# The last 2,176 bytes a row of a weight load in loads of 126, 2, 124 and 4 rows, so that the sixteen DMA engines get unequal shares

## Chip, cores, metric

One core of a Trainium2 chip; nothing else of the program runs on the others. The metric is the device time of one execution in microseconds (us), slowest core; lower is better. Engines: PE is TensorE's matmul side, DVE is VectorE, ACT is ScalarE, SP is the sync engine that issues nearly all loads. "Engine 5" means DMA engine 5 of the core's sixteen. A straggler is an engine that finishes its share of the loads clearly later than most; the "body" are the engines that are none.

## The reference

A decoding step for 8 sequences: a modulation (six vectors of 1,024 from `silu(c) @ w_mod`), attention of 32 query heads over a cache of 8,192 keys in 4 groups, and a gated MLP. Cut to what matters here:

```python
mod = (silu(c) @ w_mod).reshape(8, 6, 1, -1)            # w_mod: 1024 x 6144 bf16, 12.6 MB
h = layernorm(x) * (1 + ca) + sa
x = x + ga * attention(h, k_cache, v_cache, wq, wo)     # caches: 2 x 67 MB, wq and wo: 8.4 MB each
h = layernorm(x) * (1 + cb) + sb
x = x + gb * ((relu(h @ W_gate) * (h @ W_up)) @ W_down) # 3 x 7.3 MB
```

There are 186 MB to read for very little arithmetic.

## The kernel before

All big inputs go through one ring in on-chip memory, `arena`, with 128 rows of 128 KB. A list of loads is made up front; each is issued from SP as soon as the program has read what stood in its place.

```python
def load(key, src, n, lo):
    place[key] = lo
    stream.append((key, src, n, lo))

def pump():
    while stream:
        key, src, n, lo = stream[0]
        if P.unread("arena", lo, lo + n):
            return
        stream.pop(0)
        dst = arena[:, lo:lo + n]
        P.op("sp", lambda e, dst=dst, src=src: e.dma_start(dst, src), writes=[slot_r(lo, lo + n)], dma=True, ...)
...
load(("wm", 0), wm_src[:, 0:D], D, 0)                     # D = 1024 columns of 2 bytes
load(("wm0", 0), wm_src[:, D:24 * D], 23 * D, D)
load(("wm", 1), wm_src[:, 24 * D:48 * D], 24 * D, 24 * D) # the load that is changed
... # wq in two loads; for each of 8 sequences K in two loads and V in one; wo, W_gate, W_up
wd_parts = [(0, 14), (14, 21), (21, 25), (25, 27), (27, 28)]
for i, (r0, r1) in enumerate(wd_parts):                   # W_down, in ever smaller loads
    load(("wd", i), d_src[:, r0 * D:r1 * D], (r1 - r0) * D, VPART + r0 * D)
```

Every load has 128 rows. The matmuls of the modulation read the ring in two halves; the second half waits for `("wm", 1)`. At the end each piece of W_down has its own matmuls, then two VectorE operations and the store follow.

## Time and profile before

| | before |
|---|---|
| three timed runs | 436.43, 436.43, 436.64 us |
| profiled run, its span | 444.49, 443.1 us (state: slow) |
| DMA engines' busy share of the span in the queue of the loads | 98.9% |
| busiest compute engines | PE 59%, DVE 56% |
| bytes read | 185.63 MB |

The profile of before fell in a slow execution, 8 us longer than the timed ones. The lines that carry the argument are in the prediction. Beside the page, I read the trace's records of single DMA packets (start, duration, bytes; no engine number) and of the sixteen steps by which a load's semaphore rises, one for each engine that has finished its share.

### The profile page before, as it was taken

The numbers are of one execution on the slowest core, as the hardware profiler recorded it, in microseconds if no ns is written. First come the engines' busy times: TensorE is split into PE (matmuls) and PEld (weight loads), VectorE is DVE, ScalarE is ACT, GpSimd is POOL, SyncE is SP. The second block draws the span as 40 slices with busy tenths as digits, with TensorE's granted clock in tenths as the row PEclk, the third lists the DMA queues.
The fourth block names the chain that finished last, engine by engine and source line by source line (L and its number), as shares of the span: only waits on it lengthen the run. The fifth ranks groups of instructions, "written<-read, shape, count | busy, mean of one in ns | idle before, by whom it ended". The sixth has DMA issues, their size and how long they took to land. (4 is left out here: it accounts for less than half of the span.)

```text
span 443.1 us, 4774 instructions
## 1 busy us (share of the span) xinstructions
PE 263.3 (59%) x2139; PEld 138.0 (31%) x1979; DVE 249.0 (56%) x342; ACT 29.5 (7%) x54; POOL 8.7 (2%) x22
## 2 busy tenths in 40 slices
PE   0324336728865783886578388658838865365157
PEld 0100002218225421822542172154217215241015
DVE  0603028872985697298569729756972975421020
ACT  1100010020001002000100200010020010100000
POOL 3000000000000000000000000000000000000000
PEclk9976657978996997799599889959968996865668
DMA  9999999999999999999999999999999999999995
GB/s 367 417 355 390 404 385 426 379 417 430 467 396 420 456 444 420 429 470 390 435 476 408 423 429 467 420 423 473 399 420 426 467 455 402 452 416 419 439 414 239
DMA packets 5494, 185.74 MB, mean 419 GB/s; under 512 B 656, under 2 KB 752, under 8 KB 1136
## 3 DMA queue, kind: packets, MB, share of 16 engines
q1 hardware_dynamic: 5360, 185.61, 98.9%
q8 instruction: 5, 0.08, 0.1%
q10 hardware_dynamic: 128, 0.04, 0.0%
q14 instruction: 1, 0.01, 0.0%
HBM read 185.63 MB, written 0.02 MB: 419 GB/s over the span
## 5 line engine op out<-in xcount | busy, mean ns | idle before, releaser
L576 DVE STREAM_TRANSPOSE kt<-arena 128x1024 uint32<-128x1024 uint32 x128 | 148.2, 1211 | 64.4 <-DVEq L181 47.3
L586 PE MATMUL ps<-kt,qpad 128*128 128x512 bf16 x512 | 133.9, 384 | 44.1 <-DVE kt L576 38.1
L626 PE MATMUL ps<-arena,pT 128*64 128x256 bf16 x1024 | 74.5, 320 | 51.8 <-PEq L181 51.8
L626 PEld LDWEIGHTS ps<-arena,pT 128*64 128x64 bf16 x1024 | 72.0, 132 | 53.7 <-issue 53.1
L586 PEld LDWEIGHTS ps<-kt,qpad 128*128 128x128 bf16 x512 | 40.5, 98 | 133.7 <-DVE kt L576 101.0
L616 DVE TENSOR_SCALAR pT<-pd,mqf 128x1024 bf16<-128x1024 bf16 x64 | 28.2, 503 | 0.6
L608 ACT ACTIVATE prb<-ps,bias 128x1024 bf16<-128x1024 f32 x16 | 17.7, 1109 | 139.8 <-DVE mjt L603 139.8
L614 DVE STREAM_TRANSPOSE pd<-prb 128x1024 bf16<-128x1024 bf16 x16 | 19.8, 1239 | 10.9 <-ACT prb L608 10.9
L592 DVE TENSOR_REDUCE negm<-ps 128x1 f32<-128x512 f32 x32 | 21.2, 661 | 4.5 <-PE ps L586 4.5
L744 PE MATMUL ps<-arena,hT 128*32 128x448 bf16 x128 | 11.1, 535 | 16.8 <-DMA arena<-in_B_W_up_dram 11.4
L751 DVE TENSOR_TENSOR kt<-ps,kt 128x448 bf16<-128x448 f32 x2 | 1.2, 618 | 27.6 <-PE ps L744 27.6
L514 PE MATMUL ps<-arena,hT 128*32 128x512 bf16 x96 | 10.3, 615 | 9.7 <-DMA arena<-in_w_mod_dram 9.7
L538 PE MATMUL ps<-arena,hT 128*32 128x512 bf16 x64 | 7.2, 631 | 14.6 <-DMA arena<-in_A_wq_dram 14.6
L645 ACT ACTIVATE oacc<-ps 128x32 f32 (+1 forms) x9 | 1.8, 197 | 159.4 <-PE ps L640 159.4
L521 DVE COPY mod<-ps 128x512 f32<-128x512 f32 x2 | 1.3, 670 | 19.3 <-PE ps L514 19.3
L567 POOL TENSOR_TENSOR qpad<-qR,mq 128x128 bf16<-128x128 bf16 x8 | 4.9, 608 | 319.2 <-DVE pT L616 260.8
L549 DVE CAST kt<-ps 128x512 bf16<-128x512 f32 x1 | 0.7, 691 | 18.2 <-PE ps L538 18.2
L744 PEld LDWEIGHTS ps<-arena,hT 128*32 128x32 bf16 x64 | 2.4, 140 | 25.7 <-DMA arena<-in_B_W_up_dram 12.0
L763 PE MATMUL ps<-arena,hmT 128*32 128x256 bf16 x112 | 8.3, 309 | 3.5 <-DVE hmT L754 3.1
L714 PE MATMUL ps<-arena,kt 128*32 128x256 bf16 x128 | 5.9, 373 | 5.1 <-DMA arena<-in_A_wo_dram 5.1
L598 PE MATMUL ps<-identf,negm 128*128 128x128 f32 x16 | 3.9, 326 | 7.8 <-DVE negm L596 7.8
L763 PEld LDWEIGHTS ps<-arena,hmT 128*32 128x32 bf16 x112 | 6.5, 109 | 5.6 <-DMA arena<-in_B_W_down_dram 4.9
(87 smaller groups left out, 80.9 us busy)
## 6 DMA issues: line engine op xcount, KB each, us to landing
arena<-in_A_k_cache_dram SPq DMA_DIRECT2D x16, 4096.0 KB, 27.5
arena<-in_A_wq_dram SPq DMA_DIRECT2D x2, 4096.0 KB, 38.3
arena<-in_B_W_gate_dram SPq DMA_DIRECT2D x1, 7168.0 KB, 24.7
arena<-in_B_W_up_dram SPq DMA_DIRECT2D x1, 7168.0 KB, 27.9
arena<-in_w_mod_dram SPq DMA_DIRECT2D x1, 6144.0 KB, 33.4
arena<-in_w_mod_dram SPq DMA_DIRECT2D x1, 5888.0 KB, 17.8
arena<-in_B_W_down_dram SPq DMA_DIRECT2D x1, 3584.0 KB, 19.7
arena<-in_B_W_down_dram SPq DMA_DIRECT2D x1, 1792.0 KB, 23.6
```

The source lines that it names most:

```text
L514: fns.append(lambda e, w=w, pr=pr, j=j, kk=kk: hold(e.matmul(ps[32 * j:32 * j + 32, pr, :], hT[:, kk, :], w[:, 2 * pr:2 * pr + 2, j, :], s ...
L538: fns.append(lambda e, w=w, r=kk - r0, z=z, g=g, kk=kk: hold(e.matmul(ps[32 * g:32 * g + 32, 4 + z, :], hT[:, kk, :], w[:, r, g, z, :], st ...
L576: P.op("dve", lambda e_: e_.transpose(ktb[:, to:to + PART].bitcast(dt.uint32), arena[:, lo:lo + PART].bitcast(dt.uint32)), reads=[slot_r(l ...
L586: fns.append(lambda e_, t=t, r=r: e_.matmul(ps[:, e // 4, :].rearrange("p (c k) -> p c k", k=32), qpad[:, t * 2 + r, 24 - 8 * i:152 - 8 * ...
L592: P.op("dve", lambda e: e.tensor_reduce(negm[:, h:h + 1], ps[:, h, :], AX.X, ALU.max, negate=True), reads=[bank(h)] + (free(("ka", b)) if ...
L608: P.op("act", lambda e: e.activation(prb[:, f, :], ps[:, 2 * f:2 * f + 2, :].rearrange("p h n -> p (h n)"), ACT.Exp, bias=bias[:, 0:1], sc ...
L614: P.op("dve", lambda e: e.transpose(pd[:, f], prb[:, f]), reads=[R("prb", f, f + 1)], writes=[R("pd", 1024 * f, 1024 * f + 1024)])
L616: P.op("dve", lambda e, g=g: e.tensor_scalar(out=pT[:, f, :, :, g, :], in0=pd[:, f].rearrange("p (c i x) -> p c i x", c=32, i=2), scalar1= ...
L626: fns.append(lambda e, n=n, h=h, c_=c_, i=i, t=t: e.matmul(ps[64 * t:64 * t + 64, 5, 0:2 * Dh].rearrange("p (i d) -> p i d", d=Dh), pT[:, ...
L714: fns.append(lambda e, w=w, k=k, j=j: e.matmul(ps[32 * j:32 * j + 32, 5, 0:256], oX[:, k, :], w[:, k, j, :], start=(k == 0), stop=(k == KO ...
L744: fns.append(lambda e, w=w, kk=kk, h=h, j=j, b0=b0: hold(e.matmul(ps[32 * j:32 * j + 32, b0 + h, 0:H], hT[:, kk, :], w[:, kk, j, h, :], st ...
L763: fns.append(lambda e, w=w, r=k - r0, k=k, i2=i2, j=j: e.matmul(ps[32 * j:32 * j + 32, 4, 0:256], hmT[:, k, 1 - i2:33 - i2], w[:, r, i2, j ...
```

## The change

Intent: the engines end unequally late, and the time is that of the last one. By giving a load a number of rows that sixteen does not divide, fewer engines take part in it; so 14 and 15 are relieved and 0 to 3 loaded.

```diff
+    UNEVEN = [(832, 126), (256, 124)]
...
-        def load(key, src, n, lo):
+        def load(key, src, n, lo, dst=None):
             place[key] = lo
-            stream.append((key, src, n, lo))
+            stream.append((key, src, n, lo, arena[:, lo:lo + n] if dst is None else dst))
...
-        load(("wm", 1), wm_src[:, 24 * D:48 * D], 24 * D, 24 * D)
+        at1 = 48 * D - sum(n for n, rows in UNEVEN)
+        load(("wm", 1), wm_src[:, 24 * D:at1], at1 - 24 * D, 24 * D)
+        for n, rows in UNEVEN:
+            for lo, part in ((0, slice(0, rows)), (n // 2, slice(rows, 128))):
+                load(("wm1", n, lo), wm_src[part, at1:at1 + n], n // 2, at1 + lo, arena[part, at1:at1 + n])
+            at1 += n
```

## The prediction

> **What bounds the kernel now.** I read the page's slices first, then the table of stretches, the chain that ended last, the DMA queues, the stretch of the last loads, and last the single packets and semaphore steps of the trace.
>
> The slices show the sixteen DMA engines busy from the first to the last, while no compute engine is above 59% of the span:
>
> ```profile
> PE   0324336728865783886578388658838865365157
> DVE  0603028872985697298569729756972975421020
> DMA  9999999999999999999999999999999999999995
> ```
>
> The table of stretches (microseconds; the last two figures are the DMA share and GB/s) says at what rate:
>
> ```profile
> 8.00:33.00 25.00, 7.00 (x53) 1.71 (x21) 7.22 (x19) 1.90 (x3) 0.00 (x0) 0.91 0.97 376
> 58.00:85.00 27.00, 15.77 (x80) 5.05 (x60) 17.48 (x20) 2.08 (x3) 0.46 (x1) 0.72 1.02 396
> 110.00:350.00 240.00, 167.04 (x1218) 91.26 (x1219) 174.75 (x226) 15.18 (x31) 3.78 (x6) 0.89 1.00 435
> ```
>
> From 110 to 350 us the share is 1.00 and the rate 435 GB/s: packet follows packet on every engine, and the loads in the queue always reach past the one in flight. The first 85 us run at some 380 to 400 GB/s at the same full share: the packets themselves are longer there (49,152 bytes in 2,036 ns, 24.1 GB/s; from 110 us on 32,768 in 1,213 ns, 27.0). I hold that for something of the profiled execution: 77 us at 24.1 instead of 27.1 cost 77 x (1 - 24.1/27.1) = 8.5 us, and the profiled run took 444.49 us against 436.43 unprofiled, 8.1 more. So in the timed runs nearly everything goes at 27.1 GB/s an engine: 185.61 MB / 16 / 27.1 = 428 us, plus 1 us before the first packet, 3 us of tail, some 2 us of what follows below and the 1.4 us between the profiled run's time and its span, makes about 436.
>
> The chain's end (start, length, what) shows what a delay of one engine costs:
>
> ```profile
> 413.18 26.30 DMA arena<-in_B_W_down_dram
> 439.49 0.04 issue
> 439.53 0.61 PE ps L763 x8
> 440.14 0.02 issue
> 440.16 0.41 PE ps L763 x4
> 440.58 0.02 issue
> 440.60 0.43 DVE lu L767
> ```
>
> The chain waits for the landing at 439.49 of a piece of the last weights; the very last piece lands at 440.12, just as its matmuls' turn comes at 440.14. A load has landed when the last of its engines has landed. So the time is that of the slowest engine's whole sequence of packets, and not of the mean engine's.
>
> How unequal are they? The sixteen steps of a load's semaphore tell, though not with the engine's number. At 44.7 us all sixteen steps lie within 0.59 us. At 350 us, behind the first step: eleven more within 0.43, then 0.51, 0.91, 1.60 and 1.92 us. For the last weights: ten steps within 0.45, then 0.92, 1.61, 1.64, 1.74, 1.92 and 1.94 us. The cause stands in the queues:
>
> ```profile
> q1 hardware_dynamic: 5360, 185.61, 98.9%
> q8 instruction: 5, 0.08, 0.1%
> q14 instruction: 1, 0.01, 0.0%
> ```
>
> Five packets of 16,384 bytes, at 50.2, 104.2, 393.8, 410.5 and 436.6 us, took 0.88 to 1.12 us each, and the q14 one of 8,192 at 84.7 us took 0.36. Following packets end to start gives sixteen sequences; each of the six sits in another one, and for most of them the data packet that ran beside it is longer too (57,344 bytes in 2,666 ns instead of 2,116). Together such a fetch puts its engine back about 1.45 us for the rest of the kernel. So five engines end 1.6 to 1.94 us behind the first, one 0.92, ten within 0.45.
>
> **What the Trainium skill says.** "DMA: Bandwidth & Descriptors", section on why a DMA increments its semaphore by 16, says a load is split over the largest number up to 16 that divides its number of rows, on the lowest-numbered engines: 128 rows on 16, and so 126 on 14, 2 on 2, 124 and 4 on 4. No load of the kernel before has such a count, so its trace neither agrees nor disagrees. The same page, "Where 436 GB/s comes from", gives 435.2 GB/s for sixteen ports, 27.2 each; the trace agrees with its 27.0 to 27.1. The page's "Latency and other measured facts" has engines 7 and 15 usually slower. The trace does not show an engine that is slower all along: the three stragglers stand 0.9, 1.6 and 1.9 us back at 107 us and still at 350 us. "Runtime: NRT & Kernel Launch", "Instruction fetch mechanics", says that instructions are fetched in 16 KiB blocks; the five 16,384-byte packets agree.
>
> **The change part by part.** Removed: of the second half of w_mod, the last 2,176 of 49,152 bytes of each row; at 27.1 GB/s 80 ns a row, and 8 rows an engine make 0.64 us on all sixteen. Added, with packet times from the trace (512 bytes 27 ns, 2,048 bytes 84 ns, a semaphore step 9 ns; 1,664 bytes an estimate between them, 27 + 1152/1536 x 57 = 70 ns):
> - 126 rows of 1,664 bytes on engines 0 to 13, 9 each: 9 x 70 + 9 = 0.64 us.
> - 2 rows on engines 0 and 1: 0.08 us.
> - 124 rows of 512 bytes on engines 0 to 3, 31 each: 31 x 27 + 9 = 0.85 us.
> - 4 rows on engines 0 to 3: 0.04 us.
>
> Sum by engine, less the 0.64 removed: 0 and 1 +0.97 us (15.6 KB more in all), 2 and 3 +0.89, 4 to 13 nothing (2.4 KB less pays for nine more packet beginnings), 14 and 15 -0.64 (17.4 KB less; the 13 KB of the title are the first pair of loads alone). The total of bytes is the same, so nothing is won but balance.
>
> Moved off the path: four more issues on the sync queue, 0.33 to 0.43 us each as those in the trace, make the first wq load be issued at about 3.2 instead of 1.6 us, with 12 MB ahead of it until 34 us. TensorE waits for five semaphores instead of one before the second half of the modulation, and the last piece lands up to 1 us later. That moves the first K load's issue from 39.5 to about 40.5 us, and the queue then holds wq until 57.6 us. Later the nearest miss is a V load issued 5 us before its turn (111.7 against 116.7), so no queue runs dry. The offsets given here therefore last until the end, 400 us later, where only the largest counts.
>
> **The sum and the rivals.** The trace does not name engines, so it does not tell which of the sixteen are the stragglers. The result hangs on that.
> - *The choice of engines was made with such names in hand:* 14 and 15 are the two that end last (1.94 and 1.92), 0 to 3 are among the ten without a fetch. Then 14 and 15 come to 1.3, 0 to 3 to at most 0.45 + 0.97 = 1.42, and the next straggler, 1.74, becomes the bound: 1.94 - 1.74 = 0.2 us won, 436.2 us. Not more, because three engines other than these two stay at 1.6 and over. For it: the odd row counts and sizes look fitted to a measured imbalance. I give it 50%.
> - *A straggler is among 0 to 3.* It goes from 1.6 to 1.94 up to as much as 2.9, and the kernel loses 0.5 to 0.95 us: 436.9 to 437.4 us. For it: with five stragglers placed at random, four engines free of them are the exception (11x10x9x8 / (16x15x14x13) = 18%). Against it: the choice was hardly random. 28%.
> - *Neither:* the latest is among 4 to 13, which the change leaves alone; 436.4 us. 20%. It holds too if the fetches fall differently in unprofiled runs.
> - *The odd splits cost more than their packets:* rows in nines instead of eights could put two engines on one target port, or the small loads could start late. All their 0.26 MB is 0.6 us of DMA time, so even at half speed this adds some 0.6 us at once, perhaps to all engines. I see nothing for it in this trace, which has no such load.
> - *The compute chain in front becomes a wait:* the modulation half a microsecond or a whole one later. Against it is the 17 us of queued wq; I give it nothing.
>
> **Range and chances.** The centre is the first case, 436.2 us. The range from 435.7 (14 and 15 more of a bound in unprofiled runs than in this one, the most that 0.64 us could give) to 437.2 (a straggler loaded further) holds all but the ends of these. Two per cent is 8.7 us; none of the parts sums to 1. Within 2%: 0.985; slower 0.01 for an unknown cost of the odd splits; faster 0.005.
>
> **What would show it right or wrong.** In the changed kernel's page: the same busy DMA row; packets in q1 up by 9 x 14 + 2 + 124 + 4 = 256 data packets and 24 semaphore ones (14 + 2 + 4 + 4). 1,664-byte packets near 70 ns and 512-byte ones near 27. In the semaphore steps of the first wq load: four engines about 0.9 us later than the body, two 0.6 earlier. At the end, the last load's steps: two stragglers fewer at 1.9 if the first case holds, one at 2.5 or more if the second does. Wrong altogether would be: the semaphore steps of the odd loads spread over another number of engines, packets of 512 bytes far over 27 ns, any slice of the DMA row under 9 before the last, or a time outside 435 to 438.

## The result and the profile after

| | before | after |
|---|---|---|
| median of 6 runs, same rounds | 436.50 us (436.43 to 436.82) | 436.75 us (436.42 to 438.28) |
| ratio of fast runs | | 1.0013, 95% interval 0.9996 to 1.003 |
| profiled run | 444.49 us | 436.74 us |

A ratio is the mean time of one kernel's fast runs over that of the other's of the same rounds, so not quite the ratio of the medians. Executions over 1.5% slower than the fastest of the same kernel are left out of the means. The interval lies within 2% of 1. It also contains 1, so no difference is shown in either direction; the means differ by 0.58 us for the worse. Four of the six runs of the changed kernel lie between 436.42 and 436.75, two at 438.02 and 438.28.

The busy row and the queues of the page after:

```profile
DMA  9999999999999999999999999999999999999995
...
q1 hardware_dynamic: 5640, 185.61, 98.9%
q8 instruction: 5, 0.08, 0.1%
...
q14 instruction: 1, 0.01, 0.0%
```

The same bytes in 280 packets more: 256 of data and 24 semaphore steps, as predicted. The five 16 KB packets and the one of 8 KB are there again. The issues of the changed load (KB each, and us to landing where all sixteen steps were seen):

```profile
arena<-in_w_mod_dram SPq DMA_DIRECT2D x1, 5872.0 KB, 31.0
...
arena<-in_w_mod_dram SPq DMA_DIRECT2D x1, 204.8 KB
...
arena<-in_w_mod_dram SPq DMA_DIRECT2D x1, 62.0 KB
...
arena<-in_w_mod_dram SPq DMA_DIRECT2D x1, 3.2 KB
arena<-in_w_mod_dram SPq DMA_DIRECT2D x1, 2.0 KB
```

The four odd loads have no landing time because their semaphores did not rise in sixteen steps: the trace has 15, 3, 5 and 5 updates, the first of them at the issue, and then 14, 2, 4 and 4. That is the rule of the Trainium skill ("DMA: Bandwidth & Descriptors", why a DMA increments its semaphore by 16): 126 rows went to 14 engines, 2 to 2, 124 to 4, 4 to 4.

The stretches of the changed kernel (last two figures: DMA share, GB/s):

```profile
8.00:33.00 25.00, 6.40 (x53) 1.71 (x22) 7.22 (x19) 1.90 (x3) 0.00 (x0) 0.86 0.98 411
58.00:85.00 27.00, 18.18 (x70) 6.38 (x70) 22.02 (x26) 0.22 (x2) 0.46 (x1) 0.87 1.02 442
110.00:350.00 240.00, 167.13 (x1214) 91.15 (x1212) 174.71 (x225) 14.98 (x30) 3.77 (x6) 0.89 1.00 433
```

The first 85 us no longer run at 376 to 396 GB/s: a 46,976-byte packet of the modulation's weights takes 1,735 ns (27.1 GB/s), where the profile of before had 49,152 bytes in 2,036 ns. That is no merit of the change. The first stretch is slow in some executions of either kernel: two of before's later runs took 444.59 and 444.84 us, a run of end_before (below) that was not the profiled one took 444.80, and the trace of end_before, which keeps before's first loads, runs at 27.1 GB/s. Those slow runs left no trace; that they have the same slow stretch is inferred from their length. So the profile of before and that of after must not be subtracted.

The end of the chain after:

```profile
404.43 27.36 DMA arena<-in_B_W_down_dram
431.80 0.04 issue
431.84 0.61 PE ps L768 x8
432.45 0.02 issue
432.47 0.41 PE ps L768 x4
```

It has the same form as before: a landing of W_down, then twelve matmuls.

Two things in the packet records were not foreseen. The 32,768-byte packets of the first wq load, which follow the odd loads, take 1,276 to 1,765 ns each where they are an engine's first, and 1,213 to 1,216 from the third on. And of the sixteen steps of the last load the last comes 2.07 us behind the first; the prediction's first case has 1.74.

### The profile page after: what moved, and what is told of

Same layout as the page of the kernel before. It is cut to its first block, busy times and chain, and to the rows that moved or that the text cites. A ratio compares the mean times of both kernels' runs of the same rounds, so it can differ in the third digit from the quotient of the medians.

```text
span 435.4 us, 4780 instructions
## 1 busy us (share of the span) xinstructions
PE 260.0 (60%) x2139; PEld 138.4 (32%) x1979; DVE 248.9 (57%) x342; ACT 29.5 (7%) x54; POOL 8.7 (2%) x22
## 5 line engine op out<-in xcount | busy, mean ns | idle before, releaser
L631 PE MATMUL ps<-arena,pT 128*64 128x256 bf16 x1024 | 76.4, 325 | 51.2 <-PEq L181 51.2
L631 PEld LDWEIGHTS ps<-arena,pT 128*64 128x64 bf16 x1024 | 74.0, 134 | 53.1 <-issue 52.5
L749 PE MATMUL ps<-arena,hT 128*32 128x448 bf16 x128 | 9.2, 460 | 19.7 <-DMA arena<-in_B_W_up_dram 12.3
L519 PE MATMUL ps<-arena,hT 128*32 128x512 bf16 x96 | 9.0, 552 | 9.9 <-DMA arena<-in_w_mod_dram 9.9
L543 PE MATMUL ps<-arena,hT 128*32 128x512 bf16 x64 | 7.2, 631 | 11.6 <-DMA arena<-in_A_wq_dram 11.6
L719 PE MATMUL ps<-arena,kt 128*32 128x256 bf16 x128 | 4.9, 329 | 4.6 <-DMA arena<-in_A_wo_dram 4.6
```

The lines of the kernel that those rows point to most:

```text
L519: fns.append(lambda e, w=w, pr=pr, j=j, kk=kk: hold(e.matmul(ps[32 * j:32 * j + 32, pr, :], hT[:, kk, :], w[:, 2 * pr:2 * pr + 2, j, :], s ...
L543: fns.append(lambda e, w=w, r=kk - r0, z=z, g=g, kk=kk: hold(e.matmul(ps[32 * g:32 * g + 32, 4 + z, :], hT[:, kk, :], w[:, r, g, z, :], st ...
L631: fns.append(lambda e, n=n, h=h, c_=c_, i=i, t=t: e.matmul(ps[64 * t:64 * t + 64, 5, 0:2 * Dh].rearrange("p (i d) -> p i d", d=Dh), pT[:, ...
L749: fns.append(lambda e, w=w, kk=kk, h=h, j=j, b0=b0: hold(e.matmul(ps[32 * j:32 * j + 32, b0 + h, 0:H], hT[:, kk, :], w[:, kk, j, h, :], st ...
```

## The experiments

Three theories. **A**: the stragglers are fixed. Five engines carry the instruction fetches of 16 KB; 14 and 15 are at most two of these five, so that relieving them wins 0.2 us at most, and the engine with the 8 KB packet is among the loaded 0 to 3. **B**: 14 and 15 are really the last. **C**: the odd row counts cost DMA time by themselves, because an engine then writes rows that belong to another engine's port. Each kernel was correct against the reference. The first four kernels (two with markers in two places, pair126, pair124) ran on one chip, all the others on another; before took 436.35 and 436.36 us there (medians of fast runs).

### marks_before and marks_after: engine numbers by markers in two places

Edit, to the kernel before and to the changed one: fifteen tiny loads of 1 to 15 rows behind the first wq load and again behind the last load, each with its own row length, so that an engine's number follows from which of them it carries.

```diff
+        def mark(block):
+            for r in range(1, 16):
+                n = 16 + 8 * r
+                P.op("sp", lambda e, r=r, n=n: e.dma_start(tagt[0:r, block, r - 1, 0:n], A_wq[0:r, 0:n]), ..., dma=True, own="tag")
...
+                if key == ("wq", 0): mark(0)
+                if key == ("wd", 4): mark(1)
```

Without a wait for these loads at the end their semaphore could still rise after the program's end.

> The kernel before with 15 tiny loads of 1 to 15 rows (48 to 272 bytes a row, into memory nobody reads) queued behind the first wq load and again behind the last weights; each goes to as many engines as it has rows, so they write an engine's number into the trace. Time: within 0.5 us of before. Theory A (fixed stragglers): one of engines 14 and 15 and at least one other engine of 0 to 13 end 1.6 to 2.0 us behind the first, so freeing 14 and 15 alone can win at most 0.2 us; the engine that fetched 8,192 bytes near 80 us, 0.9 us behind here, is one of 0 to 3. Theory B (the choice was right): 14 and 15 are the two last, by 0.2 us or more.

> The changed kernel with the same markers. Theory A: 14 and 15 lead the body behind the first wq load and one of them ends first of all; one of 0 to 3 is the last at the end, by about 2.05 us behind the first, pushed over the stragglers of 4 to 13 by the 12 KB more. Theory B: the last engine is one of 4 to 13 and no engine of 0 to 3 is over 1.6 us behind.

Measured: 439.04 us (438.76 to 439.27) and 439.96 us (439.61 to 440.29) against 436.35; ratios 1.006 and 1.0082. Both miss: the markers disturb what they should measure. Their packets take 9 to 19 ns, but on engine 0 most of them in the first block stand 0.29 to 0.43 us apart, and the engines with many markers end last: in marks_before engine 0 at 434.0, engine 7 at 430.9 us. Nothing about the change follows from them, except that a markers' block may only stand behind all data.

### end_before and end_after: markers only behind the last load

Edit: the first block of markers taken out of both.

```diff
-                if key == ("wq", 0): mark(0)
```

> The kernel before with the 15 marker loads only behind the last weights, so that they name the engines and disturb no data packet. Theory A: at the end engines 14 and 15 are not the only ones 1.5 us or more behind the first; at least two of 0 to 13 are too, and the engine 0.9 us behind is one of 0 to 3. Theory B: 14 and 15 are the last two. Time about 1.5 to 3 us over before, since the output waits behind the markers.

> The changed kernel with the same markers at the end. Theory A: one of 0 to 3 is last by 2.0 to 2.1 us; one of 14 and 15 is first. Theory B: the last is one of 4 to 13. Time within 0.5 us of end_before under both.

Measured: 436.91 us (fast runs of 436.27, 436.91 and 437.07; one slow run of 444.80 left out) and 436.62 us (436.45 to 436.71) against 436.33; ratios 1.0008 and 1.0006. The markers cost almost nothing here; I had expected 1.5 to 3 us. Both profiled runs are fast, and no packet of the first loads is long, so these two traces may be compared. When each engine had its last data, read off its first marker (engine 15, which has none, from its last packet), in us:

```
engine        0      1      2      3      4      5      6      7      8      9     10     11     12     13     14     15
end_before 429.82 430.05 429.77 430.70 429.82 431.49 431.37 429.94 429.82 432.19 431.40 429.92 429.90 429.96 431.53 430.07
end_after  430.94 431.18 430.95 431.69 430.36 431.73 431.99 430.57 430.33 431.88 431.87 430.31 430.37 430.34 431.83 429.84
difference  +1.12  +1.13  +1.18  +0.99  +0.54  +0.24  +0.62  +0.63  +0.51  -0.31  +0.47  +0.39  +0.47  +0.38  +0.30  -0.23
```

Four things follow.

1. The stragglers are 5, 6, 9, 10 and 14 (1.6 to 1.8 us behind the first; engine 9 more, see 4) and, less, 3. They are the same six in both kernels, and they fit the five instruction packets of 16 KB and the one of 8 KB. Engine 15 is no straggler: in the changed kernel it ends first and idles for two microseconds.
2. Engine 14 was the last in end_before, had engine 9 not had its bad start, but only 0.04 us after engine 5, 0.13 after 10, 0.16 after 6. Whatever it is relieved of, the time of this execution can fall by 0.04 us.
3. Engines that the change was to leave alone end 0.4 to 0.6 us later. That is theory C's cost, below. It takes most of what 15 was given: -0.23 instead of -0.64 us.
4. One engine or another loses up to 1 us in the first loads, at random: in end_before one step of the first loads' semaphores is 0.98 us late from 17 us on. By the numbers this is engine 9, whose 16 KB packet then made it 2.4 us late; its -0.31 is this accident. Such a start would move an end by more than the whole change, when it falls on a straggler.

For the last: in end_after it is engine 6, with 9, 10, 14, 5 and 3 within 0.3 us. Theory A said one of 0 to 3. In end_after that is wrong; in the changed kernel's own trace it is right: there the engine that was hit by the 8 KB packet at 78 us is, its packets followed back end to start, one with 31 packets of 512 bytes, so one of 0 to 3, and it is 1.2 us late before that packet and 2.04 to 2.17 after, up to the end. So engine 3 was raised among the last, as one of six. The expectation of 0.5 us between the kernels' times held.

The chain's ends of the two, end_before first:

```profile
404.96 26.94 DMA arena<-in_B_W_down_dram
431.89 0.04 issue
...
432.57 0.41 PE ps L772 x4
```

```profile
404.51 27.20 DMA arena<-in_B_W_down_dram
431.71 0.04 issue
...
432.40 0.41 PE ps L777 x4
```

Without engine 9's accident the end before would be engine 14's 431.53 and after it is 431.99: 0.46 us later by the traces.

### pair126 and pair124: one pair of odd loads alone

```diff
-    UNEVEN = [(832, 126), (256, 124)]
+    UNEVEN = [(832, 126)]        # pair126
+    UNEVEN = [(256, 124)]        # pair124
```

> The first pair of loads alone (last 1,664 bytes a row in 126 and 2 rows): 14 and 15 get 13 KB less, no engine over 3.3 KB more. Theory A: no gain, since stragglers among 0 to 13 keep the end: 436.3 to 436.6, no engine of 0 to 3 last. Theory B (14 and 15 bind): 0.2 us or more faster than before. Theory C (odd rows collide at the target ports): slower than before by 0.2 us or more although no engine gets 2 us of work more, and the first wq packets of the other engines take over 1,213 ns.

> The second pair alone (last 512 bytes a row in 124 and 4 rows): 0 to 3 get 12 KB more, all others 4 KB less. Theory A: as slow as the changed kernel or slower, 0.2 to 0.6 us over before, one of 0 to 3 last. Theory B: equal to before within 0.2 us. Theory C: first wq packets over 1,213 ns on engines 4 to 15 while 0 to 3 still write small rows, at least 0.2 us each.

Measured: pair126 436.60 us (436.43 to 437.76), ratio 1.0005 (0.9992 to 1.0019); pair124 436.30 us (436.12 to 437.44), ratio 1.0007 (0.9993 to 1.002). No gain from relieving 14 and 15; this alone does not refute theory B, since the collisions in pair126 (below) could eat a gain of 0.2 us. There is no clear loss in either, so theory A's 0.2 to 0.6 us for pair124 is not seen. An estimate from the numbers above says why: engine 3 ended at 430.70 in end_before; 31 + 1 packets of 27 ns instead of 8 rows of 19 add 0.71 us, which makes 431.41, still under the 431.53 of engine 14, and the other five are relieved of 4 KB. In the packets: the first wq packets take 1,460 to 1,638 ns in pair126 (1,213 on none), and 1,213 to 1,251 in pair124, whose 512-byte packets all take 27 ns. So theory C holds for the nines of 126 rows and not, at this size, for the 124 rows alone.

The 437.76 us of pair126 was the profiled run, and its trace shows why: from 7 to some 19 us its packets of the first loads run at 24.1 to 24.7 GB/s instead of 27.1, 2.28 us of packet time an engine over the full rate in the whole run, against 0.69 in pair124. It looks like a short piece of the slow stretch that made before's profile 8 us long. That this is also behind the changed kernel's runs of 438.0 and 438.3 us is likely and not shown: timed runs leave no trace.

### even128 and even64: as many small packets, without imbalance

```diff
-            for lo, part in ((0, slice(0, rows)), (n // 2, slice(rows, 128))):
-                load(("wm1", n, lo), wm_src[part, at1:at1 + n], n // 2, at1 + lo, arena[part, at1:at1 + n])
+            load(("wm1", n, 0), wm_src[:, at1:at1 + n], n, at1)      # even128
```

```diff
-    UNEVEN = [(832, 126), (256, 124)]
+    UNEVEN = [(832, 64), (256, 64)]                                  # even64
```

> The same last 832 and 256 columns in two loads of 128 rows each: as many small packets, no imbalance. Theory C (nines of rows collide at the target ports): first wq packets at 1,213 ns, no cost. If small packets as such slow the neighbours: first wq packets over 1,300 ns. Time 436.1 to 436.6, as before, under all: 9 more packet beginnings an engine are about 0.15 us.

> The last 832 and 256 columns in loads of 64 and 64 rows: by the skill's rule every one of the four goes to all 16 engines, 4 rows each, so every engine gets what it got before and none is idle, but an engine no longer writes the rows that it writes in a 128-row load. Theory C1 (rows written by another engine than in a 128-row load collide with that engine's writes): small packets and first wq packets over 1,213 ns, as in the changed kernel's 1,640 to 1,750. Theory C2 (it is the idle engines or the 124 small packets on four that disturb): 1,213 ns as in even128. Time 436.2 to 436.9.

Measured: even128 436.73 us (436.31 to 437.05), ratio 1.0006 (0.9993 to 1.002); even64 437.14 us (436.83 to 437.23), ratio 1.0015 (1.0002 to 1.0029), the one light variant with an interval that leaves out 1. Of the ten fast runs of before that it is compared with, one alone (436.67 us) is of its own session. Both medians lie over what was expected, by 0.1 and 0.2 us. The durations of small packets and of each engine's first wq packet, in ns:

```
            1,664 bytes        512 bytes          first wq packet of 32,768
even128     69 to 69           27 to 27           1,213 on all sixteen
pair124     -                  27 to 27           1,213 to 1,251
pair126     69 to 98           -                  1,460 to 1,638
even64      up to 124          27 to 58           1,352 to 1,686
changed     67 to 146          27 to 69           1,276 to 1,765
```

The same shows in the profile. The stretch from 30 to 34 us, each kernel's line for end_before, even128, even64 and end_after in turn (last two figures: DMA share, GB/s; a stretch that cuts packets has shares over 1):

```profile
30.00:34.00 4.00, 1.89 (x20) 0.28 (x8) 0.00 (x0) 0.00 (x0) 0.00 (x0) 0.50 0.89 385
```

```profile
30.00:34.00 4.00, 2.10 (x21) 0.34 (x9) 0.00 (x0) 0.00 (x0) 0.00 (x0) 0.50 1.11 463
```

```profile
30.00:34.00 4.00, 1.21 (x12) 0.32 (x8) 0.00 (x0) 0.00 (x0) 0.00 (x0) 0.50 1.17 430
```

```profile
30.00:34.00 4.00, 1.07 (x12) 0.32 (x8) 0.00 (x0) 0.00 (x0) 0.00 (x0) 0.50 1.16 430
```

Divide the rate by the share to see what a busy DMA engine moves: 385 / 0.89 = 433, 463 / 1.11 = 417, 430 / 1.17 = 368, 430 / 1.16 = 371 GB/s. The engines were no less busy in the last two, they moved less while busy. Summed over the packets that start between 30 and 40 us, less their usual durations (those of even128), the cost is 0.53 us of packet time an engine in even64, 0.52 in the changed kernel, 0.35 in pair126, 0.02 in pair124. even64 gives every engine exactly the bytes of before, and no engine is left out of any of its loads (sixteen steps each); it still costs what the changed kernel costs. So it is neither idle engines nor small packets as such, but which engine carries which rows. That fits the Trainium skill, "DMA: Bandwidth & Descriptors", the descriptor swizzle: in a load of 128 rows each engine writes the partitions of one port of the memory. With 64 or 126 rows the split cannot be that one, and two engines would meet at a port. The packet records name neither rows nor ports, so the meeting itself is inferred. An engine that carries other rows also reads other addresses of the source, and no run here tells the reading side from the writing side. That the cost follows the split of the rows is shown.

### heavy124: four times the second pair

```diff
-    UNEVEN = [(832, 126), (256, 124)]
+    UNEVEN = [(1024, 124)]
```

> The second pair alone with 1,024 columns instead of 256: engines 0 to 3 get 48 KB more (31 x 2,048 + 2,048 - 8 x 2,048 bytes), the rest 16 KB less. By the packet durations 0 to 3 come 32 x 0.081 - 8 x 0.076 = 2.0 us later, the rest 0.6 us earlier. Theory A (slowest engine's sequence is the time, the 8 KB straggler of 0.9 us among 0 to 3): end at about 0.9 + 2.0 = 2.9 behind the old first instead of 1.9, so 0.8 to 1.2 us slower than before. If offsets were made up by later loads: no slower than pair124.

Measured: 438.83, 439.06, 441.43 and 441.67 us against 436.33; ratio 1.0101 (1.0076 to 1.0125). The loaded engines stay late until the end, 330 us later: at 91 us and at 364 us the last step of a V load comes 3.43 and 3.36 us behind the first. Nothing levels it out, as theory A has it. The size was missed. The imbalance is about as expected (3.36 us, behind a first engine that was itself relieved of 0.6), but slower packets came on top: the first two wq packets of the twelve other engines took 1,508 to 2,320 ns, which makes 1.3 us of packet time an engine over pair124 (1.96 against 0.69). With the 0.8 to 1.2 us expected that gives 2.1 to 2.5, near the 2.5 and 2.7 of the two runs at 439. What separates the two runs at 439 from the two at 441.5 is not known; the trace is of the run of 438.83.

### tail126 and tail123: the same tool at the end, and on the right engines

Edit: the kernel before, with the last load of W_down (1,024 columns), or its last 384 columns, in odd loads.

```diff
+            odd = r1 * D - 1024 if i == 4 else r1 * D       # tail123: - 384
...
+            if i == 4:
+                for j, part in enumerate((slice(0, 126), slice(126, 128))):      # tail123: 123
+                    load(("wdo", j), d_src[part, odd:r1 * D], 512, VPART + odd + 512 * j, arena[part, VPART + odd:VPART + r1 * D])
```

> The kernel before with its last load of all (one row block of w_down, 2,048 bytes a row) in 126 and 2 rows: 14 and 15 are relieved of all 16 KB of it (0.65 us), 0 to 13 get one packet more (0.08 us), and nothing is loaded after it. Theory A (five stragglers 5, 6, 9, 10, 14): no gain, 0 to 0.15 us slower than before. Theory B (14 and 15 bind): 0.3 us or more faster.

> The kernel before with the last 384 columns of that last load in 123 and 5 rows: by the skill's rule 0 to 2 get 41 rows of 768 bytes (1.3 us) and all sixteen are relieved of 8 rows of 768 bytes (0.25 us), stragglers included; 0 to 2 had no fetch and 1.5 us to spare. Theory A: the last lands 0.2 to 0.25 us earlier, 436.1 against 436.35, and 0 to 2 end at 1.0 to 1.3 us behind the first. If collisions at the end eat it: no gain, and packets of the last loads longer than 81 ns for 2,048 bytes.

Measured: tail126 436.48 to 437.31 us in its five fast runs (one slow run of 447.36 left out), ratio 1.001 (0.9997 to 1.0023); tail123 436.20, 436.47, 436.62 and 436.68 us, one run of 441.16 that counts as fast and one slow one of 447.13, ratio 1.0029 (0.9991 to 1.0066). tail126 has no gain, but its packets of 2,048 bytes take up to 147 ns instead of 84, so that a gain could have been eaten here too: against theory B stands the table of end_before, and these two runs only agree with it. tail123 relieves the real stragglers and has none either. Two reasons show in its trace. The fourth W_down load, beside whose last packets the leading engines already write the odd rows, landed 1.38 us after the third, instead of 1.20 in end_before. The packets hardly show why (the longest of 1,280 bytes took 65 ns instead of 55, those of 768 all 36, so the sign named in the expectation did not come), but from 430.4 us on a semaphore step came 0.42 to 0.64 us after its packet, and 0.28 to 0.44 before. Collisions in the tail would fit this; it is not shown. And TensorE was then the bound, not the DMA. The stretch of W_down's matmuls and the last of them in the timeline, first for end_before (in the stretch, first figure after the length: PE busy; third from the end: granted clock; in the timeline: start, length, what, and the idle time before it):

```profile
424.00:432.00 8.00, 7.20 (x102) 6.17 (x104) 0.00 (x0) 0.00 (x0) 0.00 (x0) 0.82 0.81 327
```

```profile
431.94 1.03 PE L772 MATMUL ps<-arena,hmT 128*32 128x256 bf16 x12 [0.15 <-DMA arena<-in_B_W_down_dram]
```

And for tail123:

```profile
424.00:432.00 8.00, 8.00 (x100) 6.02 (x98) 0.00 (x0) 0.00 (x0) 0.00 (x0) 0.66 0.79 325
```

```profile
423.57 9.15 PE L770 MATMUL ps<-arena,hmT 128*32 128x256 bf16 x112 [3.27 <-DMA arena<-in_B_W_down_dram]
```

At a granted clock of 0.66 the 112 matmuls took 9.15 us without a wait and ended at 432.72, 0.74 us after the last landing at 431.98; at 0.82 they waited for landings and ended at 432.97. With the 0.04 and 0.41 us that the last four matmuls of end_before need after their release, the landing alone would have allowed an end at 432.4. So in an execution with a low clock at the end some 0.3 us of DMA time are hidden behind TensorE. The profiled run of even128 ended in the same way (clock 0.65, 9.17 us without a wait).

No version beat before; the best of them, pair124, is at 436.30 against 436.35.

## Why the prediction was right, and where it was not

The measured 436.75 us lies within 435.7 to 437.2, and "within 2%" had 0.985. That it does is in part luck: the upper end of the range was meant for a straggler loaded further, the lower for a gain, and the loss that the traces show came from a third thing, which had been dismissed. The frame of the argument held: the time is the slowest engine's sequence of packets, offsets survive 400 us of a full queue, and the tail behind the last landing does not change. The centre of 436.2 us rested on a case that did not happen.

- *Split of the rows on 14, 2, 4 and 4 engines:* right, by the semaphore steps. Packets in the queue up by 256 and 24: right.
- *Durations:* right where nothing disturbs (69 for an estimated 70 ns, 27 for 27 in even128). In the changed kernel itself packets of 1,664 bytes took up to 146 ns and those of 512 up to 69. "Packets of 512 bytes far over 27 ns" was one of the prediction's own signs of being wrong, and it came for part of them; so did "a time outside 435 to 438", in two of six runs (438.02 and 438.28).
- *Sizes:* two slips without weight. The odd rows hold 128 x 2,176 bytes = 0.28 MB, not 0.26, and the "title" with 13 KB is not the one of this document.
- *Sum by engine.* The engines 4 to 13 were the term that failed: "nothing", measured +0.24 to +0.63, engine 9's accident left out. 0 to 3: +0.89 to +0.97 predicted, +0.99 to +1.18 measured. 15: -0.64 predicted, -0.23 measured; 14 should have come out like it and ended 0.30 later instead, which I can't take apart from its start. The missing 0.2 to 0.6 us of engines 4 to 13 and 15 is for the most part the first wq packet: 1,641 to 1,727 ns on twelve engines instead of 1,213. On the loaded four it took 1,314 to 1,402, and they miss 0.10 to 0.29. I had this as the fourth rival ("two engines on one target port ... even at half speed this adds some 0.6 us") and dismissed it since no load of before had such a split; its size was right, its chance was not.
- *First case (50%), "14 and 15 are the two that end last":* wrong. 14 is a straggler, 15 is not; 5, 6, 9 and 10 are. 0.04 us was to be won from 14, not 0.2. That the sizes "look fitted to a measured imbalance" was an argument not from the trace, and it carried half the chances.
- *Second case (28%), a straggler among 0 to 3:* half right in its premise, wrong in its size. The straggler there is engine 3, the one with 0.9 us, not one of 1.6 to 1.94; so it came up to the others (431.69 to 431.99 in end_after) and passed them only in some traces, and the loss was not 0.5 to 0.95 us.
- *The compute chain in front:* right, nothing came of it. The second half of the modulation's matmuls starts at 32.93 us in end_after and 32.11 in end_before, and the first K load is issued at 37.34 and 37.45.
- *The slow first 85 us as "something of the profiled execution":* not so. The twelve other profiled runs do not have it at this length, and a run of end_before that was not the profiled one took 444.80 us; so it is a state of some executions. The arithmetic (8.5 us) was right.

Added up, the traces say 0.46 us slower; the timed rounds say 0.25 by medians and 0.58 by means, with an interval of -0.2 to +1.3 us (0.9996 to 1.003). Both are consistent with each other and with no change at all. The relief of 14 is worth 0.04 us, the odd splits cost about 0.5 us of packet time an engine, and the random start of an engine (up to 1 us) and TensorE's clock at the end are large enough to cover the rest.

## What to carry to other kernels

Before balancing DMA engines, find out by number which engine ends last and how far the second is behind it: relieving one of five equal stragglers wins only the distance to the next. Loads of 126 or 64 rows changed here which engine carries which rows, and most of the cost fell on the next load's packets (1,352 to 1,765 ns instead of 1,213 for the first ones, those of the loaded engines less); so look at the durations of the next load, not only at the odd load's own. Numbers of engines can be had by marker loads with growing row counts, but only behind all data.

## What the Trainium skill lacked or had wrong

- "DMA: Bandwidth & Descriptors" and "SBUF — State Buffer" say how the rows of a load are shared out and what one load reaches by itself, but neither has what a load with another split than that of 128 rows costs the load behind it: the next load's first packets of 32,768 bytes took 1,352 to 1,686 ns after loads of 64 rows and 1,460 to 1,638 after one of 126, against 1,213 after loads of 128 rows.
- "DMA: Bandwidth & Descriptors", "Latency and other measured facts", has engines 7 and 15 as usually slower; its best guess at the cause applies only to loads issued from GpSimd, and those of this kernel are issued from SP. So it is not contradicted, but it does not carry over: in end_before 7 and 15 are within 0.3 us of the fastest (429.94 and 430.07, fastest 429.77); late are 5, 6, 10 and 14 by 1.6 to 1.8 us, 9 by 2.4 (a bad start in it), and 3 by 0.9.
- "Runtime: NRT & Kernel Launch" calls crossing a 16 KiB instruction block mostly hidden. In this kernel, bound by DMA, it is not: each of the five 16,384-byte packets took about 0.9 to 1.1 us of one engine's time and put it back some 1.45 us, and it never caught up.
- No page has the slow first stretch: packets at 24.1 instead of 27.1 GB/s for up to 77 us in the slow execution that was traced, 8 us longer than the others of the same kernel (444.49 against 436.43 us); what brings it about is open.
- No page has what markers on few engines cost in mid-stream: packets of 9 to 19 ns stood 0.29 to 0.43 us apart on engine 0, and the kernel took 2.6 us more.
